# Attention output split straight into the tokens' tiles, and the first MoE's output weight converted where its factors are made

## The chip, the cores and the metric

One NeuronCore of a Trainium2 chip runs the whole program in one launch. The metric is the device time of one execution in microseconds; for the kernel before it is 955.79 us, the median of three runs (955.52 to 956.56).

## The reference, cut to what matters

Attention over 4 batches, 8 heads, 576 positions, head size 64, with a decay from the cumulative log of f, causal; its output, transposed to 2304 tokens by 512, goes through two MoE layers of width 2048 without routing. The MoE weights arrive as 64-bit floats, all else as float32.

```python
scores = where(causal, -1e9, scale * q @ k.T + cum[:, :, :, None] - cum[:, :, None, :])
attn = softmax(scores)                       # 4 x 8 x 576 x 576
x = (attn @ v).transpose(0, 2, 1, 3).reshape(2304, 512)
h = x @ moe_w_in                             # 512 -> 2048
x = (h * clip(h + 3, 0, 6) / 6) @ moe_w_out  # 2048 -> 512
h = x @ moe2_w_in
out = (max(h, 0) + log1p(exp(-abs(h)))) @ moe2_w_out
```

## The kernel before, in words

**Numbers.** Products of the MoE layers keep float32 accuracy by splitting each operand into a high part, rounded to the matmul's float32r type by ScalarE, and a low part, the difference, by VectorE or GpSimd; a product is three matmuls (high x high, high x low, low x high). A 64-bit weight tile is turned to float32 in three steps (raw_weights, lines 855 to 895): ScalarE scales the upper word (889), VectorE shifts the lower (891) and combines both (892). Three of the four MoE products (the second of the first MoE and both of the second) use a 2 x 2 scheme with seven products instead of eight, so weights are first made into seven factors, high and low, by weights(m, o, p): unit p covers two 128-row tiles of the weight, its sums are on line 932, its splits on 961 and 964, and it lies in tile U[p].

**Stages.** (1) Attention, by pairs of heads, 16 pairs, four per batch: scores (s_job, line 616, contraction of 64 rows for each head), a running minimum on VectorE (638), exponentials on ScalarE (647), transposes on TensorE (t_job, 710, four groups TP0 to TP3 per head; the first tile of 64 rows is in TP3), copies (732), the product with v (pv_job, 757), and the norm into xs (765). (2) Woven with it, the first product of the first MoE in five blocks of 512 tokens (step_g, 1008; the last has 256), evicted by 1013 and 1014; blocks 0 to 2 run beside the attention, 3 and 4 after it. (3) The second product (step_c, 1256). (4) The second MoE's first product (step_a, 1112). (5) Its second (step_b, 1311), nine blocks of 256 tokens; each block sums over eight p into four banks, which combine (1226, 1229) adds up before the store of the output (1327).

**Where x goes.** A block of tokens lies in one of two halves of MX, XG(t) with t modulo 2, high and low parts. A batch has 576 tokens and a block 512, so blocks and batches are shifted. Only for batch 0 are the first 512 tokens split from xs right away (772, 773). Every pair's xs is stored whole to x_dram (774); load_g (985) fetches blocks 1 to 4 from there, and 991 and 992 split them.

**Weights.** Two staging tiles st[0], st[1] serve all conversions during the attention, in the order in which the operations are created: 16 tiles of moe_w_in (weights_g), 16 of moe_w_out, and 16 of moe2_w_in, the latter two stored as float32 to wf_dram (899) and loaded again by weights (920). Two more staging tiles and U[1], U[2] exist once the attention's tiles are closed (open_m2). U[3] to U[7] hold the first product's weights until its last blocks have read them.

**Order.** Nothing is left to run-time scheduling. Each operation has a due time `at`, worked out from the numbers in PLAN; Work.order simulates the engines with assumed costs, gives every operation an engine, a bank and a place in its engine's queue, and each engine runs its queue in that order. All DMAs but a few are issued by SP. So a changed cost or due time moves the order of everything.

```python
best_way: min over engines of begin + cost
next op of an engine: among those that can start earliest, the one with the least `at`
```

Of the kernel before, what the change touches and what calls it, by code (L numbers as in the profile page):

```python
# [13 lines left out]
P = 128  # L14
# [37 lines left out]
    pc=78.633,  # L52
    pp=1626.916,
    pv=0,
    bend=[1.119, 1.0, 1.0, 0.9],
    b0=47.858,
    T0=59.215,
    D1=96.614,
    D2=81.65,
    D3=81.326,  # L60
    D4=70.932,
    gap=16.562,
    gap2=18.0,
    gap3=23.337,
    cA=1.111,
    SA=5.521,
    SC=4.964,
    SB=2.386,
    iva=9.172,
    nwarm=18,  # L70
    sp=0.871,
    evb=-0.48,
    u0=6.93,
    u1=47.121,
    u2=5.548,
    u3=2.95,
    fx=-1.856,
    ul=20.0,
    c1=9.498,
    c2=13.359,  # L80
    c3=23.635,
    cvw=0,
    ldw=48.152,
    xa=-3.322,
    xs=-1.161,
    ga=4.306,
    tsp=-10.459,
    xat=36.251,
    xl=1.582,
    rel=32.858,  # L90
    wfrom=7.28,
    lv0=7.543,
    lq1=4.785,
    decst=1.735,
    capH=5,
# [3 lines left out]
    slv=0,  # L99
    lat=1.649,  # L100
# [200 lines left out]
def attention_two_moe_kernel(  # L301
# [295 lines left out]
    def s_job(pn, i, idx, at):  # L597
# [27 lines left out]
        for ti, a, c, o, q0, r, y, _, _ in todo:  # L625
            for h in heads:
                par, bk = sets[h], bks[h, y]
                if c == q0 + r:
                    def hide(h=h, q0=q0, r=r):
                        blk = T["W"][z][h][:r, q0:q0 + r]  # L630
                        nc.gpsimd.affine_select(out=blk, in_=blk, compare_op=ALU.is_ge, fill=-1e9 / scale, base=0, pattern=[[-1, r]], channel_multiplier=1)  # L631

                    op(("pool", 2.0 * r + 40, hide), w=[("W", z, h, ti)], at=at, name="hide")
# [51 lines left out]
    def t_job(pn, i, idx, at):  # L685
# [26 lines left out]
        op(("pe", 109.0 * len(blocks), go), r=list(rd), w=[bk], banks=[bk], at=at, name=f"TP{idx}",  # L712
# [26 lines left out]
    def pv_job(b, hp, idx, at):  # L739
# [58 lines left out]
    def attention():  # L798
# [10 lines left out]
        for n in range(len(specs) + 1):  # L809
            for i in range(2):  # L810
# [16 lines left out]
                if not cur:  # L827
                    return
                if i == 0:
                    if n + 1 < len(specs):  # L830
                        load_v(*specs[n + 1], when(0.9))
                else:
# [6 lines left out]
                prev = (*specs[n], i)  # L839
# [137 lines left out]
    def load_g(t, at):  # L977

        a0, n = GB[t]
        done = 0  # L980
        while done < n:
            b, o = divmod(a0 + done, S)
            cnt = min(n - done, S - o)
            for c in range(NC):
                dma(lambda b=b, o=o, cnt=cnt, done=done, c=c: nc.sync.dma_start(out=XG(t)[1][:, c, done:done + cnt].bitcast(F32), in_=x_dram[b][c, :, o:o + cnt]),
                    4 * P * cnt, r=[("xd", b, c)], w=[("X", t % 2, c)], at=at + 0.1 * c, name="loadx")
            done += cnt
        for c in range(NC):
            def xt(c=c):
                return [x[:, c, 0:n] for x in XG(t)]  # L990
            op(("act", act(n, False), lambda xt=xt: nc.scalar.activation(out=xt()[0], in_=xt()[1].bitcast(F32), func=ACTF.Copy)), w=[("X", t % 2, c)], at=at + 0.1 * c, name="xh")
            op2(either(n, lambda e, xt=xt: e.tensor_tensor(xt()[1], xt()[1].bitcast(F32), xt()[0].bitcast(F32), op=ALU.subtract)), w=[("X", t % 2, c)], at=at + 0.1 * c, name="xl")
# [458 lines left out]
```

## Time and profile before

| | us |
|---|---|
| median of three runs | 955.79 |
| the profiled execution, device time | 956.72 |
| its span | 954.9 |
| TensorE busy in the span | 929.1 |
| VectorE busy | 698.9 |
| ScalarE busy | 541.5 |
| GpSimd busy | 100.8 |
| DMA, MB moved | 185.95 |

Busy times count instructions that run on an engine; matmuls are pipelined, so a busy TensorE is not one at its peak. A row of the view by stretches gives the busy time of the engines in one stretch with the count of instructions in brackets, the TensorE clock that was granted (1.00 is full), the share of time in which the DMA engines were busy and the rate. In a timeline, square brackets give the idle time ahead of an instruction and what ended it.

### The profile page before, as it was taken

To read this page: it belongs to the slowest core of one execution; us is meant where nothing else is said; L and a number is where in the kernel's file an instruction comes from. 1 tells how busy PE (TensorE), PEld (TensorE's weight loads), DVE (VectorE), ACT (ScalarE), POOL (GpSimd) and SP (SyncE) were. 2 spreads that over 40 slices of the span, in tenths; PEclk is the share of its full clock that TensorE was granted. 3 is DMA by queue.
4 is the path that set the end of the run, shared out by engine and by line. 5 is a ranking of instruction groups with operands and counts; after the bars stand their busy time and mean duration, and the time that the engine had idled before them with its cause. 6 is when DMAs were issued, how large, how long until landed. Compare 5 with 4: busy or idle time off the path is not lost.

```text
span 954.9 us, 18734 instructions
## 1 busy us (share of the span) xinstructions
PE 929.1 (97%) x6772; PEld 827.2 (87%) x6772; DVE 698.9 (73%) x1548; ACT 541.5 (57%) x1082; POOL 100.8 (11%) x238
## 2 busy tenths in 40 slices
PE   7989999989999999999999999999999999999997
PEld 5657667766767788899999999999999999999997
DVE  6757666556566478599898799969635888887785
ACT  5868666656567655453454355867666754333341
POOL 4322111111111011002003101000000000000000
PEclk9999999999999999999999999999999999999999
DMA  9897988896987798654634366699724544443441
GB/s 184 195 203 191 249 218 220 214 272 200 238 248 252 243 311 265 225 163 147 185 117 155 111 199 181 214 364 314 250 100 152 183 161 134 151 137 112 133 134 67
DMA packets 205982, 185.95 MB, mean 195 GB/s; under 512 B 105344, under 2 KB 152576, under 8 KB 205888
## 3 DMA queue, kind: packets, MB, share of 16 engines
q1 hardware_dynamic: 203264, 184.38, 65.3%
q8 instruction: 53, 0.87, 0.4%
q10 hardware_dynamic: 2624, 0.37, 0.3%
q14 instruction: 41, 0.34, 0.1%
HBM read 120.07 MB, written 64.63 MB: 193 GB/s over the span
## 4 chain that ended last, share of the span: by engine, by line
PE 73%; DVE 11%; DMA 9%; ACT 3%; issue 2%; SPq 1%; POOL 0%; ACTq 0%; DVEq 0%; POOLq 0%
PE bank L1008 19%; PE bank L1311 19%; PE bank L1112 14%; PE bank L1256 10%; PE bank L710 4%; PE bank L757 3%; PE bank L616 3%; DVE XO L1213 3%; DMA st<-in_moe_w_out_dram 2%; DVE U L964 2%; DMA GR<-g_dram 2%; DMA st<-in_moe_w_in_dram 2%; DMA kr<-in_k_dram 1%; DVE HY L1229 1%; ACT pt L732 1%
## 5 line engine op out<-in xcount | busy, mean ns | idle before, releaser
L1008 PE MATMUL bank<-MX,U 128*128 128x512 f32 (+1 forms) x960 | 235.7, 387 | 3.7 <-DVE stats L638 2.4
L1008 PEld LDWEIGHTS bank<-MX,U 128*128 128x128 f32 x960 | 158.8, 190 | 39.9 <-issue 9.0
L1311 PE MATMUL bank<-U,MX 128*128 128x256 f32 x1512 | 179.9, 281 | 0.0
L1311 PEld LDWEIGHTS bank<-U,MX 128*128 128x128 f32 x1512 | 179.6, 189 | 0.0
L1256 PE MATMUL bank<-XO,U 128*128 128x256 f32 x1344 | 159.2, 280 | 0.5 <-DVE XO L1213 0.5
L1256 PEld LDWEIGHTS bank<-XO,U 128*128 128x128 f32 x1344 | 158.4, 189 | 0.9 <-DVE XO L1213 0.7
L1112 PE MATMUL bank<-MX,U 128*128 128x288 f32 x672 | 92.4, 297 | 1.3 <-ACT HY L1128 0.9
L1112 PEld LDWEIGHTS bank<-MX,U 128*128 128x128 f32 x672 | 90.3, 188 | 2.7 <-ACT HY L1128 1.4
L1112 PE MATMUL bank<-XO,U 128*128 128x288 f32 x672 | 91.7, 297 | 0.2 <-DVE HY L1131 0.2
L1112 PEld LDWEIGHTS bank<-XO,U 128*128 128x128 f32 x672 | 90.4, 188 | 0.7 <-DVE HY L1131 0.5
L1013 ACT ACTIVATE HY<-bank,half 128x512 f32<-128x512 f32 x80 | 50.0, 641 | 49.1 <-PE bank L1008 44.2
L631 POOL TENSOR_SCALAR_AFFINE_SELECT w<-w 128x128 f32<-128x128 f32 (+1 forms) x160 | 51.6, 326 | 238.2 <-DVE stats L638 126.1
L732 ACT ACTIVATE pt<-bank 128x384 f32<-128x384 f32 (+2 forms) x127 | 58.8, 496 | 29.5 <-PE bank L710 26.8
L1014 DVE SCALAR_TENSOR_TENSOR HY<-HY,bank 128x512 f32<-128x512 f32 x80 | 49.4, 631 | 35.0 <-ACT HY L1013 34.1
L1131 DVE TENSOR_TENSOR HY<-HY,bank 128x288 f32<-128x288 f32 x96 | 42.9, 450 | 36.3 <-PE bank L1112 34.8
L1128 ACT ACTIVATE HY<-bank 128x288 f32<-128x288 f32 x128 | 50.4, 406 | 27.2 <-PE bank L1112 26.8
L616 PE MATMUL bank<-KT,QT 64*128 64x288 f32 (+4 forms) x384 | 59.9, 424 | 2.9 <-DVE QT L570 1.3
L964 DVE TENSOR_TENSOR U<-st,U 128x1024 fp32r<-128x1024 f32 (+1 forms) x48 | 52.8, 1113 | 5.0 <-ACT U L961 4.9
L961 ACT ACTIVATE U<-st 128x1024 fp32r<-128x1024 f32 (+1 forms) x48 | 45.0, 948 | 19.5 <-DVE st L932 9.9
L1153 ACT ACTIVATE HY<-HY 128x576 f32<-128x576 f32 x64 | 43.7, 684 | 20.5 <-DVE HY L1131 17.0
L616 PEld LDWEIGHTS bank<-KT,QT 64*128 64x128 f32 x384 | 32.1, 187 | 26.5 <-issue 8.0
L1209 ACT ACTIVATE MX<-GR 128x768 fp32r<-128x768 f32 x36 | 30.2, 838 | 42.0 <-PE bank L1311 42.0
(147 smaller groups left out, 1303.3 us busy)
## 6 DMA issues: line engine op xcount, KB each, us to landing
GR<-g_dram SPq DMA_DIRECT2D x72, 512.0 KB
g_dram<-HY SPq DMA_DIRECT2D x32, 576.0 KB
st<-in_moe_w_in_dram SPq DMA_DIRECT2D x32, 512.0 KB
g_dram<-HY SPq DMA_DIRECT2D x64, 256.0 KB
st<-in_moe_w_out_dram SPq DMA_DIRECT2D x32, 512.0 KB
wf_dram<-st SPq DMA_DIRECT2D x48, 256.0 KB
st<-wf_dram SPq DMA_DIRECT2D x48, 256.0 KB
w<-dec_dram SPq DMA_DIRECT2D x30, 288.0 KB
```

The costliest lines, as they stand in the source:

```text
L616: nc.tensor.matmul(bank[bks[h, y].i][:, o:o + c - a], T["Q"][z][h * D:h * D + D, q0:q0 + P], T["K"][z][h * D:h * D + D, a:c], start=lead, ...
L631: nc.gpsimd.affine_select(out=blk, in_=blk, compare_op=ALU.is_ge, fill=-1e9 / scale, base=0, pattern=[[-1, r]], channel_multiplier=1)
L732: e.activation(out=place(i, j, a, c), in_=src(), func=ACTF.Copy)
L961: op(("act", act(n * h, False), lambda src=src, to=to: nc.scalar.activation(out=to(0), in_=src(), func=ACTF.Copy)), r=rd, w=w, at=at, name ...
L964: e.tensor_tensor(to(1), src(), to(0).bitcast(F32), op=ALU.subtract)
L1008: nc.tensor.matmul(bank[bk.i][:, 0:n], w, x, start=(c == 0 and y == 0), stop=(c == NC - 1 and y == 2))
L1013: op(("act", act(n, True, 1) + 10, lambda: nc.scalar.activation(out=g, in_=bank[bk.i][:, 0:n], func=ACTF.Relu, scale=1.0 / 6.0, bias=half) ...
L1014: op(("dve", dve(n), lambda: nc.vector.scalar_tensor_tensor(out=g, in0=g, scalar=1.0, in1=bank[bk.i][:, 0:n], op0=ALU.min, op1=ALU.mult)), ...
L1112: nc.tensor.matmul(bank[bks[b].i][:, 0:HA], wa[u][:, c], xa[v][:, c], start=(nm in ("P1", "P2", "P5") and c == 0 and y == 0), stop=(c == 1 ...
L1128: op(("act", act(HA, True) + 30, lambda: nc.scalar.activation(out=to(q), in_=bp(), func=ACTF.Copy)), r=new, banks=[ba], w=[("H", i, q)], a ...
L1256: nc.tensor.matmul(bank[bks[b].i][:, o * 256:(o + 1) * 256], *ops, start=(p == 0 and o == 0 and y == 0), stop=(p == NPR - 1 and y == 2), s ...
L1311: nc.tensor.matmul(bank[bks[b].i][:, o * 256:(o + 1) * 256], ga[u], wa[v], start=(p == 0 and o == 0 and y == 0), stop=(p == NPR - 1 and y ...
```

## The change

Six things change, and with them the order of all operations, since it is worked out anew.

1. Each pair's output is split from xs straight into the block of its batch: batch b's first 512 - 64 b tokens go to the block b, high by ScalarE and low by VectorE or GpSimd. Only the remaining 64 (b + 1) tokens are stored to x_dram, and load_g fetches them for block b + 1 in two transfers (three of the four column groups, then the last). A half of MX now has two keys for each column group, for the part from xs and for the part from DRAM, and every product of the block reads both. To keep the dependencies in order, attention is a generator that yields after each batch, and the block's products are created between.
2. moe_w_out is no longer converted into wf_dram during the attention; weights(0, 1, p) loads the 64-bit tiles and converts them in the staging tiles ahead of its sums.
3. The first tile's transposes use 64 rows and a 64 x 64 identity instead of 128 x 128; the planner's cost for one is 55 ns instead of 109.
4. In the last block of stage 5 the products of the last two p are interleaved (P1 of both, P6 of both, ...), and its output is stored in three parts: one row half whole, the other in two halves of 128 KB.
5. The first weight's loads are created ahead of the attention, so they no longer follow the store of the decays.
6. Most numbers of PLAN change; the planner's cost of one causal mask on GpSimd rises by 50 ns.

```diff
 PLAN = dict(
...
-    b0=47.858,
+    b0=45.976,
     T0=59.215,
-    D1=96.614,
-    D2=81.65,
+    D1=102.897,
+    D2=77.724,
...
-    u1=47.121,
+    u1=49.035,
...
-    ldw=48.152,
+    ldw=37.258,
...
-    capH=5,
+    capH=4,
...
-    lat=1.649,
+    lat=2.309,
 )
...
             for p0, ti, k0 in blocks:
-                nc.tensor.transpose(acc[:, p0:p0 + P], T["P"][par][ti][:, k0:k0 + P], ident)
+                r = CUT[ti][1]
+                nc.tensor.transpose(acc[:, p0:p0 + r], T["P"][par][ti][0:r, k0:k0 + P], ident[0:r, 0:r])
...
-        if b == 0:
-            xh, xl = (XG(0)[z][:, hp] for z in range(2))
-            op(("act", act(TB, False), lambda: nc.scalar.activation(out=xh, in_=X()[:, 0:TB], func=ACTF.Copy)), r=xk, w=[("X", 0, hp)], at=at - K["xat"], name="xh")
-            op2(either(TB, lambda e: e.tensor_tensor(xl, X()[:, 0:TB], xh.bitcast(F32), op=ALU.subtract)), r=xk, w=[("X", 0, hp)], at=at - K["xat"], name="xl")
-        dma(lambda: nc.sync.dma_start(out=x_dram[b][hp], in_=X()), 4 * P * S, r=xk, w=[("xd", b, hp)], at=at, name="storex")
+        o, n = S * b - TB * b, TB * (b + 1) - S * b
+        xh, xl = (XG(b)[y][:, hp, o:TB] for y in range(2))
+        op(("act", act(n, False), lambda: nc.scalar.activation(out=xh, in_=X()[:, 0:n], func=ACTF.Copy)), r=xk, w=[("X", b % 2, hp, 0)], at=at - K["xat"], name="xh")
+        op2(either(n, lambda e: e.tensor_tensor(xl, X()[:, 0:n], xh.bitcast(F32), op=ALU.subtract)), r=xk, w=[("X", b % 2, hp, 0)], at=at - K["xat"], name="xl")
+        dma(lambda: nc.sync.dma_start(out=x_dram[b][hp, :, n:S], in_=X()[:, n:S]), 4 * P * (S - n), r=xk, w=[("xd", b, hp)], at=at, name="storex")
...
     def load_g(t, at):
-        a0, n = GB[t]
...
+        b = t - 1
+        s0 = TB * t - S * b
+        n = S - s0
+        for c0, c1 in ((0, NC - 1), (NC - 1, NC)):
...
+                nc.sync.dma_start(out=XG(t)[1][:, c0:c1, 0:n].bitcast(F32), in_=x_dram[b][c0:c1, :, s0:S].rearrange("c p s -> p c s"))
...
-            op(("pe", 3 * 119.0, go), r=[("unit", p, group(fz))] + [("gf", 1, i, 3 * (az > 2), s) for s in range(2)], w=[bks[b]], banks=[bks[b]], at=mb_at(t, p, x / 7), name="b" + nm,
+            op(("pe", 3 * 119.0, go), r=[("unit", p, group(fz))] + [("gf", 1, i, 3 * (az > 2), s) for s in range(2)], w=[bks[b]], banks=[bks[b]], at=mb_at(t, p, x / 7) if t < NT // NG - 1 or p < NPR - 2 else mb_at(t, NPR - 2, (2 * x + p % 2) / 7), name="b" + nm,
...
-        for h in range(2):
+        cuts = [(1, 0, 2), (0, 0, 1), (0, 1, 2)] if t == NT // NG - 1 else [(0, 0, 2), (1, 0, 2)]
+        for h, y0, y1 in cuts:
...
-    converts(0, 1, BLK[1] - K["c1"], BLK[2] - K["c1"], 2)
+    pass
     converts(1, 0, BLK[2] - K["c2"], BLK[3] - K["c2"], 2)
...
+    for t in attention():
...
-    weights(0, 1, 0, c_at(0, 0) - K["u1"] - 30, 0, False)
+    weights(0, 1, 0, c_at(0, 0) - K["u1"] - 30, 0, True)
...
-        weights(0, 1, p, c_at(0, p) - K["u1"] - 15, p % 2 * 2, False)
+        weights(0, 1, p, c_at(0, p) - K["u1"] - 15, p % 2 * 2, True)
```

## Rows read from the trace of the kernel before

**Rows 1.** Busy time by stretches: attention (two), the rest of stage 2, stage 3
```profile
20.00:140.00 120.00, 110.64 (x720) 76.60 (x718) 81.20 (x267) 88.57 (x243) 28.18 (x76) 0.97 0.86 211
140.00:340.00 200.00, 196.30 (x1213) 142.98 (x1210) 116.03 (x339) 126.77 (x319) 25.22 (x78) 0.99 0.83 236
340.00:400.00 60.00, 60.00 (x344) 52.33 (x344) 44.36 (x89) 29.39 (x49) 5.90 (x3) 1.00 0.85 282
400.00:580.00 180.00, 179.06 (x1500) 177.56 (x1499) 162.40 (x289) 85.63 (x105) 17.52 (x18) 1.00 0.50 152
```
**Rows 2.** The same view in steps of 20 us
```profile
120.00:140.00 20.00, 18.18 (x96) 12.54 (x96) 11.20 (x37) 13.26 (x36) 3.04 (x9) 0.91 0.82 228
```
**Rows 3.** Timeline of TensorE, instructions behind an idle stretch
```profile
131.59 0.33 PE L710 MATMUL bank<-ident,p3b 128*128 128x128 f32 x1 [1.82 <-DVE stats L638]
...
197.30 1.65 PE L1008 MATMUL bank<-MX,U 128*128 128x512 f32 x3 [2.39 <-DVE stats L638]
```
**Rows 4.** Chain of waits: start, us, what
```profile
190.36 5.82 DMA st<-in_moe_w_out_dram
...
230.27 6.52 DMA st<-in_moe_w_out_dram
```
**Rows 5.** DMA view, 20 to 340 us
```profile
DMA packets 119086, 72.43 MB, mean 226 GB/s; under 512 B 85837, under 2 KB 100356, under 8 KB 119050
...
st<-in_moe_w_in_dram SPq DMA_DIRECT2D x24, 512.0 KB
...
st<-in_moe_w_out_dram SPq DMA_DIRECT2D x16, 512.0 KB
```
**Rows 6.** Timeline of VectorE: a norm, the next batch's first, a split after its load
```profile
164.20 0.49 DVE L765 TENSOR_TENSOR xs<-bank,ivb 128x320 f32<-128x320 f32 x1
...
181.51 0.43 DVE L765 TENSOR_TENSOR xs<-bank,ivb 128x256 f32<-128x256 f32 x1
182.47 0.69 DVE L992 TENSOR_TENSOR MX<-MX 128x512 fp32r<-128x512 f32 x1 [0.53 <-ACT MX L991]
```
**Rows 7.** Timeline of SP's issues: the last loads of x for block 1
```profile
175.94 1.00 SPq L985 DMA_DIRECT2D MX<-x_dram  x2
```
**Rows 8.** Timeline of ScalarE: the last eviction of block 0
```profile
161.19 0.69 ACT L1013 ACTIVATE HY<-bank,half 128x512 f32<-128x512 f32 x1 [0.39 <-PE bank L1008]
```
**Rows 9.** Stretches, instructions of line 892 alone: VectorE busy, clock, DMA
```profile
140.00:285.00 145.00, 11.03 (x16) 0.99 0.85 229
285.00:400.00 115.00, 12.41 (x18) 1.00 0.81 268
```
**Rows 10.** Groups by form: busy us, mean ns of one, idle before
```profile
L891 DVE TENSOR_SCALAR st<-st 128x512 uint32<-128x512 uint32 x64 | 27.4, 428 | 24.7 <-DMA st<-in_moe_w_in_dram 12.5 <-DMA st<-in_moe_w_out_dram 12.2
```
**Rows 11.** Stretches in stage 3, columns as in rows 1
```profile
420.00:460.00 40.00, 39.06 (x325) 38.30 (x324) 38.43 (x70) 18.69 (x22) 5.13 (x5) 1.00 0.55 171
460.00:500.00 40.00, 40.00 (x342) 40.00 (x341) 35.30 (x64) 19.68 (x26) 0.74 (x1) 1.00 0.45 134
```
**Rows 12.** Chain of waits: G matmuls behind scores, between transposes; transposes alone
```profile
107.00 0.90 PE bank L1008 x3
...
122.50 0.70 PE bank L1008 x3
...
329.61 0.33 PE bank L710 x3
```
**Rows 13.** Groups by form: weight loads of the scores and of transposes
```profile
L616 PEld LDWEIGHTS bank<-KT,QT 64*128 64x128 f32 x384 | 32.1, 187 | 26.5 <-issue 8.0 <-DVE stats L638 8.0 <-ACT pt L732 4.3
...
L710 PEld LDWEIGHTS bank<-ident,pc 128*128 128x128 f32 x120 | 14.2, 142 | 7.7 <-DVE stats L638 2.6 <-DVE xs L765 1.6 <-issue 0.8
```
**Rows 14.** Timeline of the tail, all engines
```profile
943.79 5.72 PE L1311 MATMUL bank<-U,MX 128*128 128x256 f32 x47
...
948.56 2.75 DVE L1229 TENSOR_TENSOR HY<-HY,bank 128x256 f32<-128x256 f32 x7 [5.96 <-ACT HY L1226]
951.00 0.81 SPq L1327 DMA_DIRECT2D out_dram<-HY  x2
```

More of the change, by code (lines that the diff above doesn't have):

```diff
@@ L98 @@
     slp=0,
-    slv=0,
-    lat=1.649,
+    slv=26.051,
+    lat=2.309,
 )
@@ L709, in go @@
             for p0, ti, k0 in blocks:
-                nc.tensor.transpose(acc[:, p0:p0 + P], T["P"][par][ti][:, k0:k0 + P], ident)
-        op(("pe", 109.0 * len(blocks), go), r=list(rd), w=[bk], banks=[bk], at=at, name=f"TP{idx}",
+                r = CUT[ti][1]
+                nc.tensor.transpose(acc[:, p0:p0 + r], T["P"][par][ti][0:r, k0:k0 + P], ident[0:r, 0:r])
+        op(("pe", sum(109.0 if CUT[b[1]][1] == P else 55.0 for b in blocks), go), r=list(rd), w=[bk], banks=[bk], at=at, name=f"TP{idx}",
            after=[("PT", i, t[0], t[1]) for t in todo])
@@ L826, in attention @@
                         pv_job(*prev[:2], idx, at - K["tsp"])
-                if not cur:
-                    return
-                if i == 0:
+                if cur and i == 0:
                     if n + 1 < len(specs):
                         load_v(*specs[n + 1], when(0.9))
-                else:
+                elif cur:
                     inv_job(n, when(1.0) - K["iva"])
@@ L977, in load_g, with xt @@
     def load_g(t, at):
-        a0, n = GB[t]
[L980 to L992, printed above, removed]
+        b = t - 1
+        s0 = TB * t - S * b
+        n = S - s0
+        for c0, c1 in ((0, NC - 1), (NC - 1, NC)):
+            k = [("X", t % 2, c, 1) for c in range(c0, c1)]
+            dma(lambda c0=c0, c1=c1: nc.sync.dma_start(out=XG(t)[1][:, c0:c1, 0:n].bitcast(F32), in_=x_dram[b][c0:c1, :, s0:S].rearrange("c p s -> p c s")),
+                4 * P * n * (c1 - c0), r=[("xd", b, c) for c in range(c0, c1)], w=k, at=at, name="loadx")
+            def xt(c0=c0, c1=c1):
+                return [x[:, c0:c1, 0:n] for x in XG(t)]
+            m = n * (c1 - c0)
+            op(("act", act(m, False), lambda xt=xt: nc.scalar.activation(out=xt()[0], in_=xt()[1].bitcast(F32), func=ACTF.Copy)), w=k, at=at + 1, name="xh")
+            op2(either(m, lambda e, xt=xt: e.tensor_tensor(xt()[1], xt()[1].bitcast(F32), xt()[0].bitcast(F32), op=ALU.subtract)), w=k, at=at + 1, name="xl")
     ngb = [0]
@@ L1008, in go @@
                     nc.tensor.matmul(bank[bk.i][:, 0:n], w, x, start=(c == 0 and y == 0), stop=(c == NC - 1 and y == 2))
-            op(("pe", 3 * (0.4495 * n + 3.2), go), r=[("W1", ft, 0), ("W1", ft, 1), ("X", t % 2, c)], w=[bk], banks=[bk], at=at, name=f"G{t}.{ft}", seq="s" if c == 0 else None)
+            op(("pe", 3 * (0.4495 * n + 3.2), go), r=[("W1", ft, 0), ("W1", ft, 1)] + [("X", t % 2, c, y) for y in range(2)], w=[bk], banks=[bk], at=at, name=f"G{t}.{ft}", seq="s" if c == 0 else None)
         g = HY[0][:, i * TB:i * TB + n]
@@ L1332, in attention_two_moe_kernel @@
         op(("pe", 213.0, lambda: nc.tensor.matmul(bank[0][:, 0:P], ident, ident)), r=["ident"], w=[wb], banks=[wb], at=-10.0, name="warm")
-    attention()
-    last_att = list(wk.ops)
+    for ft in range(NF):
+        weights_g(ft)
     wk.mark = ()
@@ L1370, in attention_two_moe_kernel @@
             freed(on_tile[made], [("unit", made, 0), ("unit", made, 1)])
-            weights(0, 1, made, c_at(0, made) - K["u1"], made % 2 * 2, False)
+            weights(0, 1, made, c_at(0, made) - K["u1"], made % 2 * 2, True)
             made += 1
-    freed([("X", z, c) for z in range(2) for c in range(NC)], xkeys("M"))
+    freed([("X", z, c, y) for z in range(2) for c in range(NC) for y in range(2)], xkeys("M"))
     freed([("g", i) for i in range(4)], obs)
```

80 lines of the change are left out of this document (42 added, 38 removed).

## The prediction

> **What bounds the kernel now.** The execution behind the profile took 956.72 us on the device, 954.9 of them span; the median of the runs shown is 955.79, so I work out a difference and put it on both. First I read the stretches by stage [rows 1]. From 400 us on TensorE is never free for more than a per cent: 179.06 busy of 180 in the second products of the first MoE. 340 to 400 is full. Only the attention, woven with the first MoE's first products, has holes: 9.36 idle of 120 (20 to 140 us) and 3.70 of 200 (140 to 340), 13.1 together. A hole also costs afterwards: the 20 us with the idle stretch at 131.59 have a granted clock of 0.91, a part of them at 1.2 instead of 2.4 GHz [rows 2]; with two more such stretches (0.91 from 60 us, 0.92 from 180) that is 20 x (0.09 + 0.09 + 0.08) = 5.2 us of work (the stages' mean clocks of 0.97 and 0.99 give 5.6). So 18.3 us is the most that smoother attention could give back.
>
> Then I ask what ends the holes. The two longest after 100 us, 1.82 and 2.39 us, wait for VectorE's row statistics (line 638) [rows 3], and the chain of waits puts ahead of the second of them a load of a staged weight that takes 5.82 us; ahead of 1.30 us more at 236 to 239 stands another, of 6.52 us [rows 4]. The engine reads its queue in order: a conversion whose weight has not landed (line 891) stands in front of the attention's reductions. Between 20 and 340 us the DMA moves 72.43 MB [rows 5] and its engines are busy 0.83 to 0.86 of the time [rows 1]. This is a stage where TensorE has little slack and DMA decides where it waits.
>
> **The x path.** Before, a pair's normed output goes to DRAM and comes back. For the last pair of the second batch the norm ends at 164.69, the last loads are issued at 175.94, and the low part of the split starts at 182.47 [rows 6, 7]: 18 us, in which the next G block can only hold open banks. After, ScalarE and VectorE split straight out of xs; of 0.69 us each at 512 columns these two instructions were paid before too, only after the load, so their sum is nil: 24 pairs of instructions instead of 20, each shorter. What goes is DMA: stores of 576 tokens per batch become 64 (b+1), so 2304 x 2048 B = 4.72 MB become 640 x 2048 B = 1.31, and loads of 1792 tokens (3.67 MB) become 1.31: 5.8 MB less, and SP issues 16 + 8 transfers instead of 16 + 28. What is late next is the split's own dependency: batch b writes the half of MX that block b-2 read. Batch 2's first pair is normed at 181.51, 20 us after the last eviction of block 0 begins [rows 6, 8], so I cost that wait at nothing; if cover went, an ACT queue with exponentials behind it would wait.
>
> **The weight path.** 16 conversions of moe_w_out (loads of 512 KB, conv on ACT and DVE, store and reload of 256 KB each) leave the attention [rows 5]. Their place, 140 to 285 us, held 16 of the combining steps; the stretch 285 to 400 held 18, those of moe2_w_in [rows 9]. Staging has two buffers and is filled in order of creation, so moe2_w_in should move up into the vacated place, and moe_w_out comes after it, at the factors. VectorE there gets 16 x (0.43 + 0.69) = 17.9 us [rows 9, 10] and loses 18 x the same = 20.1: about nil, beside 15.6 us free in 340 to 400 [rows 1]. 8.4 MB of traffic, the store and reload of 16 x 256 KB, disappears. With x, and with 16 conversions fewer before 340 (where 40 ran, 16 of w_out and 24 of w_in [rows 5]; now some 34, as unit 0 and a few more come early), the attention moves about 72.4 - 5.8 - 6 x 0.5 - 8 x 0.26 = 61.5 MB, 15% less.
>
> How much of the holes that closes I can't read off; the bounds are 0 and 18.3. The waits that end in a staged load or stand right behind one are 1.82 + 2.39 + 1.30 = 5.5 us, and two of the three stretches of low clock follow them (1.8 + 1.6): 8.9. As the conversions of moe2_w_in now stand where those of moe_w_out stood, the in-order wait itself stays, only the load is shorter; I take half, **-4.5 us**.
>
> Block 0 of the second products needs a unit of factors every 5 us (42 matmuls of 0.117, by 342 in 40 us). At 420 to 460 it ran 325 matmuls where the next 40 us ran 342 [rows 11]: 17 x 0.117 = 2.0 us lost now, with VectorE 38.43 of 40 busy. Units 0, 2, 4 and 6 hung on buffers that moe2_w_in held until 392; they can now be early, but each takes a load of twice the bytes and 2.24 us of VectorE more. Between -2 and +4 us; **-0.5**.
>
> **The half-height transposes.** 32 blocks (one in each group TP3) become 64 rows by 64 columns moving instead of 128. Full ones take 0.11 us each (0.33 for three) [rows 12]. If time went by moving columns alone, 32 x 0.055 = 1.7 us go. Against it: three G matmuls take 0.70 us between transposes, but 0.90 next to the scores' 64-row matmuls, with the same 512 columns [rows 12]: going into another row shape and back costs 0.19 to 0.20 us. A 64-row block within 128-row work pays that too: 32 x (0.19 - 0.055) = +4.3 us; if nothing is saved either, 32 x 0.19 = +6.1. From -1.7 to +6.1; some of the blocks already stand next to scores or PV and pay half. The nearest row is the 64-row scores, so I take **+3.5 us**, on TensorE's path, since in this stage nothing hides it.
>
> Whether even the 0.055 are saved depends on the weight load. Scores load 64 x 128 in 187 ns, transposes 128 x 128 in 142 [rows 13]: half the rows don't load faster. The Trainium skill, in "TensorE: Matmul & The Clock Gate", section "LDWEIGHTS (loading the stationary operand)", says the same: the time goes by columns, not by the contraction rows. By that rule the half block's load is as long as before, the saving is nil and the total 2.6 us worse than mine.
>
> **The tail.** The last matmul ends at 949.51, VectorE's seven additions end at 951.31, two stores are issued from 951.00 to 951.81 [rows 14]. They start late because bank 0 closes only 5 x 0.357 us before the end (five more products of three matmuls, 0.119 each by the same row's 47). Interleaved, P1 and P6 are complete 10 x 0.357 = 3.6 us before it, five additions lie beside matmuls, and one of 0.4 remains behind the last. The last store is issued near 950.0 instead of 951.4, and is half as large: **-1.5 us** (-0.8 to -2.2). It needs the last unit's factors one step earlier, and they are there: in the last 6 us no matmul waits.
>
> **Sum.** -4.5 - 0.5 + 3.5 - 1.5 = -3.0 us: 953.7 against the profiled 956.72, 952.8 against the median.
>
> **Rivals.**
> (a) The transposes cost what their columns say: -4.5 - 0.5 - 1.7 - 1.5 = -8.2, 947.6. For it: the transposes' load is shorter than others' [rows 13]. Against it: 0.70 and 0.90 [rows 12].
> (b) The half transposes save nothing and pay every switch, +6.1: -4.5 - 0.5 + 6.1 - 1.5 = -0.4, 955.4; no change. The section named above stands behind the first half of it.
> (c) Slower: the row-shape switches, +4.3 for all 32, with nothing from the DMA's relief, because moe2_w_in's conversions block VectorE just where moe_w_out's did: +4.3 - 1.5 = +2.8, 958.6. It decides once the relief is under 0.9 us. For it: order and planner's constants are new everywhere, and holes elsewhere may open.
> (d) The units come late: moe2_w_in does not move up, 17.9 us go onto 340 to 400, where 15.6 are free; 2.3 spill into block 0, where each lost step shows, beside the 2.0 lost there: +4 in place of -0.5, 957.3.
>
> **Chances and range.** Mine 0.40, (a) 0.17, (b) 0.10, (c) 0.20, (d) 0.13. What a measurement of this kernel tells from no change is about 0.2%, 1.9 us: 953.9 and 957.7. Faster: most of mine (0.32), (a), a little of the others: 0.54. Same 0.22. Slower: (c) and half of (d), and what of mine goes wrong: 0.24. My own case spans 948 to 956. The range reaches from below (a), with two thirds more relief, to above (c) with +6.1: 945 to 961.
>
> **What would show it.** Relief: TensorE's idle time from 20 to 340 falls from 13.1 towards 9, loads of staged weights get shorter, the granted clock dips less often. Weights: conversions of moe2_w_in end before 320, those of moe_w_out lie from there to 430, and 420 to 460 holds 325 matmuls or more. Transposes: G matmuls or transposes next to a 64-row block start about 0.1 us later than next to a full one; if the spacing falls to 0.055 with no gap, (a). Tail: last store's issue within 1 us of the last matmul. The prediction is wrong if a new hole of over 3 us opens in the attention, if block 0 starves, or if G matmuls wait on the x split.

## The result and the profile after

The changed kernel takes 962.89 us, the median of four runs; the kernel before took 955.65 in the same session. The ratio is 1.0073, with an interval of 1.0046 to 1.0099: slower by 7 us, where 3 us less were forecast, and outside the range. The profiled execution took 962.57 us, 960.8 of them span: 5.9 more than the span before. The differences below are made on these two executions.

First the stretches, with the columns of [rows 1]: us, busy time and count of TensorE, weight loads, VectorE, ScalarE and GpSimd, granted clock, DMA share, GB/s.

```profile
20.00:140.00 120.00, 115.23 (x722) 79.67 (x719) 85.57 (x274) 90.96 (x250) 25.84 (x73) 0.95 0.81 196
140.00:340.00 200.00, 194.77 (x1194) 138.39 (x1192) 111.16 (x334) 121.58 (x312) 24.43 (x79) 0.98 0.68 192
340.00:400.00 60.00, 57.36 (x316) 48.47 (x313) 55.55 (x96) 35.59 (x55) 12.05 (x14) 1.00 0.70 232
400.00:580.00 180.00, 180.00 (x1488) 178.05 (x1487) 147.50 (x264) 78.60 (x99) 20.12 (x18) 1.00 0.47 142
```

In the second row the DMA share fell from 0.83 to 0.68 and TensorE's idle time rose from 3.70 to 5.23 us: the traffic went and the holes stayed. Idle time from 20 to 340 us is 4.77 + 5.23 = 10.0 (13.1 before), but the clock is lower in both rows: 120 x 0.05 + 200 x 0.02 = 10.0 us of work, where it was 5.6. The stretch 340 to 400 has 2.64 us of holes where it had none, with VectorE 55.55 of 60 busy instead of 44.36. In steps of 20 us, these two carry most of the lost clock [rows 2]:

```profile
20.00:40.00 20.00, 18.36 (x111) 13.09 (x109) 13.19 (x46) 13.80 (x42) 3.25 (x12) 0.79 0.86 177
220.00:240.00 20.00, 16.98 (x91) 12.09 (x89) 7.57 (x23) 8.61 (x24) 1.81 (x6) 0.83 0.81 224
```

TensorE's timeline shows what stood ahead of them, and a third hole later; these answer to [rows 3].

```profile
31.57 1.87 PE L616 MATMUL bank<-KT,QT 64*128 64x288 f32 x4 [1.27 <-DVE stats L638]
...
224.41 0.33 PE L711 MATMUL bank<-ident,p1b 128*128 128x128 f32 x1 [1.42 <-DVE stats L638]
...
227.37 0.36 PE L711 MATMUL bank<-ident,p0b 64*128 64x64 f32 x1 [1.60 <-DVE stats L638]
...
271.81 0.81 PE L616 MATMUL bank<-KT,QT 64*128 64x320 f32 x4 [1.88 <-DVE stats L638]
```

The chain of waits over 214 to 230 us answers to [rows 4]: the load is now one of moe2_w_in (the view leaves out the 2), and no shorter (5.82 and 6.52 before).

```profile
218.50 2.09 DMA wf_dram<-st
220.59 0.02 issue
220.60 6.06 DMA st<-in_moe_w_in_dram
```

VectorE's timeline shows the queue that TensorE hangs on: it stands twice at a conversion (L892), with the row statistics (L638) right behind; at 270.56 the attention's statistics stand behind the split of an x that came from DRAM (L992).

```profile
223.80 0.43 DVE L892 TENSOR_SCALAR st<-st 128x512 uint32<-128x512 uint32 x1 [2.47 <-DMA st<-in_moe_w_in_dram]
224.14 0.21 DVE L638 CUSTOM_DVE_ANT_0 pc<-bank,w 64x64 f32<-64x64 f32 x1
...
226.76 0.43 DVE L892 TENSOR_SCALAR st<-st 128x512 uint32<-128x512 uint32 x1 [2.40 <-DMA st<-in_moe_w_in_dram]
...
270.56 0.76 DVE L992 TENSOR_TENSOR MX<-MX 128x576 fp32r<-128x576 f32 x1 [4.02 <-ACT MX L991]
271.23 0.51 DVE L638 CUSTOM_DVE_ANT_0 pc<-bank,w,stats 128x288 f32<-128x288 f32 x1
```

The DMA view of 20 to 340 us [rows 5]: 10.5 MB less, as forecast (61.5 MB), with 4 loads of moe_w_out instead of 16.

```profile
DMA packets 118054, 61.89 MB, mean 193 GB/s; under 512 B 86274, under 2 KB 103682, under 8 KB 118018
...
st<-in_moe_w_in_dram SPq DMA_DIRECT2D x29, 512.0 KB
...
st<-in_moe_w_out_dram SPq DMA_DIRECT2D x4, 512.0 KB
```

The combining steps (now L893) before and after 285 us [rows 9], and the start of the second products [rows 11]:

```profile
140.00:285.00 145.00, 9.66 (x14) 0.98 0.72 197
285.00:400.00 115.00, 13.42 (x20) 1.00 0.63 206
```

```profile
420.00:460.00 40.00, 40.00 (x340) 40.00 (x339) 30.20 (x55) 15.03 (x18) 6.47 (x5) 1.00 0.40 125
460.00:500.00 40.00, 40.00 (x341) 40.00 (x340) 33.76 (x61) 19.02 (x24) 1.85 (x1) 1.00 0.53 157
```

In TensorE's timeline the starts of transposes show the 64-row blocks [rows 12]: full after full follows in 0.11 us (22.08, 22.19, 22.30), a half one behind a full one in 0.20 (22.30 to 22.50), a full one behind a half one in 0.20 (23.07 to 23.27).

```profile
22.08 0.27 PE L711 MATMUL bank<-ident,p2b 128*128 128x128 f32 x1
22.19 0.27 PE L711 MATMUL bank<-ident,p3b 128*128 128x128 f32 x1
22.30 0.27 PE L711 MATMUL bank<-ident,p4b 128*128 128x128 f32 x1
22.50 0.64 PE L711 MATMUL bank<-ident,p 64*128 64x64 f32 x3
23.07 0.27 PE L711 MATMUL bank<-ident,p0b 64*128 64x64 f32 x1
23.27 0.33 PE L711 MATMUL bank<-ident,p1b 128*128 128x128 f32 x1
```

Their weight loads, by form (busy us, mean ns), are 136 ns for 64 rows and 149 for 128 [rows 13]; the tail answers to [rows 14].

```profile
L711 PEld LDWEIGHTS bank<-ident,pc 128*128 128x128 f32 x112 | 14.0, 149 | 3.2 <-ACT pd L647 0.8
...
L711 PEld LDWEIGHTS bank<-ident,pc 64*128 64x128 f32 x8 | 1.1, 136 | 2.2 <-issue 1.1 <-ACT pt L733 1.0 <-ACT U L974 0.2
```

```profile
939.83 16.55 PE L1311 MATMUL bank<-U,MX 128*128 128x256 f32 x138
...
956.42 1.08 DVE L1229 TENSOR_TENSOR HY<-HY,bank 128x256 f32<-128x256 f32 x3 [0.33 <-PE bank L1311]
956.87 1.30 SPq L1328 DMA_DIRECT2D out_dram<-HY  x3
```

### The profile page after: what moved, and what is told of

It reads as the page before. It is cut to its first block, busy times and chain, and to the rows that moved or that the text cites. A ratio compares the mean times of both kernels' runs of the same rounds, so it can differ in the third digit from the quotient of the medians.

```text
span 960.8 us, 18597 instructions
## 1 busy us (share of the span) xinstructions
PE 938.2 (98%) x6772; PEld 831.4 (87%) x6772; DVE 702.1 (73%) x1545; ACT 543.2 (57%) x1082; POOL 108.3 (11%) x249
## 4 chain that ended last, share of the span: by engine, by line
PE 84%; DVE 6%; DMA 6%; ACT 1%; issue 1%; POOL 1%; SPq 0%; DVEq 0%; POOLq 0%; ACTq 0%
PE bank L1311 19%; PE bank L1008 18%; PE bank L1112 17%; PE bank L1256 15%; PE bank L711 6%; PE bank L616 4%; PE bank L758 4%; DMA st<-in_moe_w_in_dram 2%; DVE XO L1213 2%; DVE U L965 1%; DMA g_dram<-HY 1%; PE bank L1333 1%; DMA w<-dec_dram 1%; DMA GR<-g_dram 1%; DVE HY L1014 1%
## 5 line engine op out<-in xcount | busy, mean ns | idle before, releaser
L1008 PE MATMUL bank<-MX,U 128*128 128x512 f32 (+1 forms) x960 | 238.8, 388 | 3.0 <-DVE HY L1014 2.0
L733 ACT ACTIVATE pt<-bank 128x448 f32<-128x448 f32 (+2 forms) x123 | 58.4, 498 | 25.6 <-PE bank L711 24.7
L1209 ACT ACTIVATE XO<-GR 128x768 fp32r<-128x768 f32 x36 | 30.3, 841 | 51.1 <-PE bank L1256 35.9
L1213 DVE TENSOR_TENSOR MX<-GR,MX 128x768 fp32r<-128x768 f32 x36 | 34.7, 964 | 30.2 <-ACT MX L1209 30.2
```

The costliest lines, as they stand in the source:

```text
L733: e.activation(out=place(i, j, a, c), in_=src(), func=ACTF.Copy)
L1008: nc.tensor.matmul(bank[bk.i][:, 0:n], w, x, start=(c == 0 and y == 0), stop=(c == NC - 1 and y == 2))
L1209: op(("act", act(cnt, False), lambda src=src, dst=dst: nc.scalar.activation(out=dst(0), in_=src(), func=ACTF.Copy)), r=rd, w=[("gf", m, i, ...
L1213: e.tensor_tensor(dst(1), src(), dst(0).bitcast(F32), op=ALU.subtract)
```

## The experiments

Ratios are to the kernel before, run beside each, with 95% intervals. "Loss" is TensorE's idle time up to the end of its last PV product (the product with v), plus half of the time at 1.2 GHz there; it is 23.0 us before and 24.7 after, with the last PV product ending at 332.8 and 340.2.

Losses and ends of stages are read from one execution of each kernel, and they vary. Two pairs of kernels have the same order in every queue up to the last block: the kernel before and e9 lose 23.0 and 21.9 us, with the last PV product ending at 332.8 and 330.4; e12 and e15 lose 22.6 and 19.5, at 333.6 and 330.3. So a difference of 3 us in the loss is no difference between kernels; the ratios, from 4 to 12 runs of each, are the firmer numbers.

### The half-height transposes

The changed kernel in its own order with full transposes, and the kernel before in its own order with half ones:

```diff
-tensor.transpose(acc[:, p0:p0 + r], T["P"][par][ti][0:r, k0:k0 + P], ident[0:r, 0:r])   # e1_full: changed kernel
+tensor.transpose(acc[:, p0:p0 + P], T["P"][par][ti][:, k0:k0 + P], ident)
```

> The changed kernel with the 32 half-height transposes issued as full 128 x 128 ones again; the order of every queue is that of the changed kernel. Theory 'row shape': in the trace of the changed kernel a half block starts 0.203 us after the matmul ahead instead of 0.109, and the next full block again 0.203 after it, so 30 x 0.094 + 32 x 0.094 = 5.8 us go: 962.9 - 5.8 = 957.1, and the span of the attention (last product with v) from 340.2 to about 334.5. Rival 'columns': halving the moving columns saved 32 x 0.055 = 1.7 us and the attention is longer for another reason (new holes): 964.6. Rival 'waits take it': the attention waits on VectorE anyway, so shorter transposes only lengthen the waits: 961 to 963.

> The kernel before with the same 32 transposes at half height, nothing else, order of all queues as before. Row shape: +5.8 us, 961.4 to 961.5, if nearly all groups stand behind 128-row work. Columns: -1.7, 954. If e1 and this one agree in size with opposite signs, the term stands alone and doesn't hang on the rest of the change.

Measured: 957.53 us, 1.0022 [0.9999, 1.0045], against 1.0073 with half blocks; and 957.37, 1.0024 [1.0000, 1.0049], for half blocks alone. They cost in both directions, 0.0051 and 0.0024, the second at the edge of its interval. TensorE's work up to the last PV product (its end less the loss) grew with the half blocks by 4.9 us from e1 to the changed kernel and by 6.6 from before to e2, so in e2 part of the cost seems to have filled holes; how much, one execution can't tell (the profiled one took 954.70, the median is 957.37). And e1, which holds every other part of the change, is no faster than before: the expected gain is missing without them too.

### Is it the conversions' work?

In the changed order, VectorE's part of moe_w_out's conversion is left out and its load takes as many bytes of q (e3), then ScalarE's part too (e5), or the whole conversion of moe2_w_in (e4):

```diff
-op2(("dve", dve(n), lambda: nc.vector.scalar_tensor_tensor(
+op2(("dve", dve(n), lambda: None if (m, o) == (0, 1) else nc.vector.scalar_tensor_tensor(   # e4: (1, 0)
```

> The changed kernel in its order, without VectorE's two conversion steps of moe_w_out (32 instructions, 17.9 us of VectorE); the staged words are loaded from q in the same shape and size, so the outputs are not the reference's. Theory 'VectorE full': between 340 and 380 us it is busy 17.1 and 20.0 of 20 and G matmuls wait 2.6 us for the evictions of line 1014; without the steps these waits go and G ends 73 us after the last product with v instead of 76.7: -2.5 to -3.7 us, 959.2 to 960.4. Rival 'DMA': the evictions wait for stores of g (4.00 us in the chain of waits at 354.8) and loads of the factors, which don't change here: within 1 us of 962.9.

> The changed kernel in its order, without all three conversion steps of moe_w_out, ScalarE's too (words loaded from q in the same shape and size; outputs not the reference's). Without VectorE's two steps alone the stretch from the last product with v to the end of G stayed at 77.3 us (76.8 in the changed kernel, 73.0 before). Theory 'ScalarE's queue': G evictions (line 1013) stand behind conversions (line 890) whose 512 KB have not landed (4.1 and 1.4 us in the run with full transposes); without them the stretch falls to 73.5 to 75, the time by 2 to 3.5 us. Rival 'factor loads': VectorE and ScalarE stand at the first factors of G (loads of 6.5 to 7.5 us), which stay: the stretch stays above 76.

> The changed kernel in its order, without the three conversion steps of moe2_w_in (ACT's and VectorE's); the words are loaded from q in the same shape and size, stored and reloaded as before, so the outputs are not the reference's. Theory 'in order': the holes of 3.0 us at 224 to 227 and 2.2 at 271 to 278 and the low clock after the first (6.8 us at half) come from VectorE standing at a conversion whose weight hasn't landed; without it they go: 3.0 + 2.2 + 3.4 = -8 to -9 us, 954. Rival 'just work': only the instructions' own time goes, which TensorE does not see here: -1 to 0. Rival 'other waits': the next-latest thing in the same queue (loads of q and k, decays) ends the waits instead: -3 to -5.

Measured: 1.0061 [1.0041, 1.0081], 1.0085 [1.0062, 1.0107], 1.0080 [1.0055, 1.0104]; the changed kernel has 1.0073. Taking away work gives nothing. The stretch from the last PV product to the end of G (the first MoE's first product), 73.0 us before and 76.7 in the changed kernel, stays at 77.3 in e3 and 75.8 in e5. In e4 the holes at 224 us are gone, but one of 5.28 us stands at 263, behind the split of an x that SP began to load only at 263.19: the next wait was right behind. The lines are TensorE's and VectorE's.

```profile
268.71 1.44 PE L616 MATMUL bank<-KT,QT 64*128 64x320 f32 x4 [5.28 <-DVE stats L638]
...
267.46 0.76 DVE L992 TENSOR_TENSOR MX<-MX 128x576 fp32r<-128x576 f32 x1 [7.42 <-ACT MX L991]
```

### Is it the wait in order behind loads?

With full transposes, e6 holds the DRAM part of x of the last two blocks until the attention's planned end; e7 also lets the planner price the loads of moe_w_out at twice their bytes, e8 all staged loads; e10 is e8 without holding x.

```diff
-..., w=k, at=at, name="loadx")
+..., w=k, at=at, name="loadx", from_=BLK[3] if t > 2 else 0.0)     # e6, e7, e8
-dma(load, 8 * P * NC * P, w=[("stage", i), ("up", i)], ...
+dma(load, 16 * P * NC * P, w=[("stage", i), ("up", i)], ...         # e8, e10; e7: for (0, 1) alone
```

> The changed kernel with full transposes, and with the loads of x from DRAM for blocks 3 and 4 held in the plan until the attention's end, so that their splits leave the attention's queues (planned anew from there on). Theory 'split in the way': the hole before the scores at 268 to 272 us (2.0 us, 5.3 in the run without the conversions, there with 3.5 us of low clock after) comes from ScalarE and VectorE standing at lines 991 and 992 for a load that SP issues late behind k loads. It goes: 957.5 - 2 to 4 = 953.5 to 955.5. Rival: the reductions then wait for the next thing (decays, k): within 1 us of 957.5.

> As the run before, and the plan prices moe_w_out's staged loads at twice their bytes (5.8 us to landing instead of 4.0; the traces show 5 to 7.5), so conversions stand later in the queues of ScalarE and VectorE. If the loss after the attention is in-order waiting for loads, the stretch from the last product with v to the end of G falls from 77 to 73 to 75 and the time by 2 to 3 us against the run before. If it is the amount of work or of traffic there, it stays.

> As the run before, with all staged loads priced so, also those within the attention; the whole order is planned anew. In-order theory: the holes at 221 to 228 us behind two conversions go too, -3 us more or better. Rival: the plan's order elsewhere gets worse as loads take more of its DMA time, or the holes only move, as in the run without moe2_w_in's conversions: 0 to +4.

> The changed kernel with full transposes, and the plan prices every staged load at twice its bytes; x loads as in the changed kernel. The run that also held x back ended the attention at 330.3 us (336.4 with full transposes alone, 332.8 before) but lost 4 us waiting for x right after. Theory 'in order': the attention's holes come from conversions planned sooner than loads land; here the attention ends near 330, x is there, G takes 73 to 76: 957.5 - 5 = 951 to 953.5. Rival 'moved': the gain in the attention came from holding x back, or is lost again after it: 956 to 959.

Measured: 1.0103 [1.0081, 1.0125], 1.0073 [1.0050, 1.0095], 1.0042 [1.0027, 1.0058], 1.0017 [0.9998, 1.0037]. Prices nearer to the landing times close the holes at 221 to 271 us, and the last PV product ends at 331.6 in e10 instead of 336.4 in e1; yet the time is e1's, since 4 us went to a later stage (A, the second MoE's first product, takes 188.4 instead of 184.3). e6 moved the wait, and e7 hardly shortens it (82.8 us from the last PV product to the end of G, 84.7 in e6, where 73 to 75 were expected). In e6 TensorE stands still for 8.63 us after the attention, and ScalarE's timeline shows why, a conversion waiting for its load ahead of the split (L991) in the same queue.

```profile
344.62 0.68 ACT L890 ACTIVATE st<-st 128x512 f32<-128x512 f32 x1 [3.27 <-DMA st<-in_moe_w_out_dram]
345.95 0.68 ACT L890 ACTIVATE st<-st 128x512 f32<-128x512 f32 x1 [0.66 <-DMA st<-in_moe_w_out_dram]
346.84 0.94 ACT L991 ACTIVATE MX<-MX 128x576 fp32r<-128x576 f32 x2 [0.20 <-DMA MX<-x_dram]
```

The same pricing on the kernel before:

> The kernel before with one edit: the planner prices all loads of staged weights at twice the bytes, nearer to the 5 to 7.5 us that they are seen to take, so that conversions are placed later than their loads. If the in-order wait at a conversion is what makes the attention's holes, the holes behind staged loads (at 131 and 197 us) go and the attention ends 2 to 4 us earlier; time -1 to -3 us if the rest keeps it, 0 if it is lost again in the products behind, as it was in the changed kernel. Rival, that the holes have other releasers: attention end unchanged.

Measured: 1.0556 [1.0524, 1.0589], against the theory. The attention ends at 333.1, as before, and TensorE stands still for 51.7 us from 406: moe2_w_in's conversions, held back, run on to 450, ahead of the factors of the second products. So a later place for the conversions closes holes in one order and opens a far larger one in another; the landing time is not the cause by itself.

```profile
457.87 0.77 PE L1256 MATMUL bank<-XO,U 128*128 128x256 f32 x2 [51.74 <-issue]
```

### The parts one by one

e9 is the kernel before with the interleaved last block and the three-part store; e12 with moe_w_out converted at the factors; e15 with both; e13 is the change without its weight path and its half blocks, in the numbers that the planner had before: the x part, the tail and the order of creation (the planner's costs of a mask and of a half block stay those of the change).

```diff
-converts(0, 1, BLK[1] - K["c1"], BLK[2] - K["c1"], 2)               # e12, e15
-weights(0, 1, p, c_at(0, p) - K["u1"] - 15, p % 2 * 2, False)
+weights(0, 1, p, c_at(0, p) - K["u1"] - 15, p % 2 * 2, True)
+... if t < NT // NG - 1 or p < NPR - 2 else mb_at(t, NPR - 2, (2 * x + p % 2) / 7)   # e9, e15
```

> The kernel before with the last block's interleaved products and the output's store in three parts, nothing else; the order differs from before's only at the end. By the trace of the changed kernel the stretch behind the last product falls from 5.4 to 4.4 us and the last stage from 177.3 to 176.5: -1.0 to -1.8 of 955. Rival: the three smaller stores land no earlier: 0.

> The kernel before with moe_w_out converted at its factors, nothing else; PLAN as before, so the order is new from the first conversion on. If 16 conversions and 6 MB fewer relieve the attention: its idle and low-clock time (13.1 + 5.1 from 20 us) falls, -2 to -4 us. If they are replaced by those of moe2_w_in with the same waits and G loses 2 to 3 us after the attention behind loads (as in the changed kernel: 2.6): 0 to +2.

> The kernel before with the x path of the changed kernel (and its interleaved tail), full transposes, PLAN as before, moe_w_out through DRAM as before; the planner still counts 55 ns for a half block. If the x path alone helps: the attention ends some us before 332.8, 950 to 953 with the tail. If splits of the DRAM part stand in the attention's queues and cost holes: 955 to 959. With e12 it tells which half of the change brings the missing relief, and which the loss.

> The kernel before with two parts of the change: moe_w_out converted where its factors are made, and the last block's products interleaved with the three-part store. Full transposes, x by DRAM, the planner of before. My theory, that these two parts gain and add: alone they gave 0.9974 and 0.9979, together about 0.995, -4 to -5 us, 951 to 952; TensorE's tail near 4.7 us, attention end near 333. Rival, that the gain of the tail and that of the conversion are the same microseconds (the last units come late): 0.997 to 0.998, no more than either alone.

Measured: e9 0.9979 [0.9955, 1.0003]; e12 0.9974 [0.9955, 0.9993]; e13 1.0088 [1.0058, 1.0118]; e15 951.28 us, 0.9959 [0.9939, 0.9979]. e15 beats both kernels, and e12 alone is clear of 1. The tail alone is not (its interval reaches 1.0003), though the stretch behind the last product is 0.7 to 0.8 us shorter in both pairs that differ in it (5.40 to 4.70, 5.00 to 4.24). That the two gains add fits e15, but so does a tail worth less: the intervals of e12 and e15 overlap. The x part with its order of creation costs 8 us, with holes from 29 to 78 us and a loss of 30.6.

### The order of creation

One thing in that part was in no term of mine. The first MoE's weights are now created ahead of the attention, so that the load of block 0's first weight no longer waits for the store of the decays. In the planner that wait is not only lost, it is turned round: the load still reads the key ("dec") that the store writes, so the store, created later, waits for the load. SP's timeline has two 512 KB loads ahead of the rows of k, one before, and it issues the store and the first reload of the decays later (13.39 and 19.87 us, 9.60 and 14.65 before); the kernel after, then the kernel before:

```profile
5.80 1.14 SPq L870 DMA_DIRECT2D st<-in_moe_w_in_dram  x2
7.06 3.99 SPq L534 DMA_DIRECT2D kr<-in_k_dram  x4
...
13.39 0.44 SPq L797 DMA_DIRECT2D dec_dram<-w  x1
...
19.87 1.55 SPq L575 DMA_DIRECT2D w<-dec_dram  x2
```

```profile
5.82 0.58 SPq L869 DMA_DIRECT2D st<-in_moe_w_in_dram  x1
...
9.60 0.47 SPq L796 DMA_DIRECT2D dec_dram<-w  x1
...
14.65 0.98 SPq L575 DMA_DIRECT2D w<-dec_dram  x2
```

Giving the wait back to e1 (e16), to e13 (e17) and to the whole change (e18), and taking it from the kernel before (e21):

```diff
 def attention():
-    decays()                       # e16, e17, e18
+decays()
 for ft in range(NF):
     weights_g(ft)
-raw_weights(i, 0, 0, ft, at, ["dec"] * (ft == 0))     # e21
+raw_weights(i, 0, 0, ft, at)
```

> The changed kernel with full transposes in the same order, and the decays' store created ahead of the first MoE's weights again, so that the first weight loads wait for it as in the kernel before. Theory, that the loss of the x part sits in the start (two 512 KB loads ahead of the k and r loads, holes and half clock at 18 to 50 us): those holes go, 3 to 5 us less than the same kernel without this edit (957.5), so 953 to 955. Rival, that the split of x from xs and the DRAM part of x in the attention's queues cost it: the early holes may go, the time stays at 956 to 959.

> The kernel with the x part on its own (x split straight from xs, interleaved last block, the planner of before, moe_w_out by DRAM, full transposes), now with the decays' store ahead of the weights. Without that edit it ran at 1.0088. Theory, that the order of creation is the loss: 0.998 to 1.001, and the holes at 29 to 78 us are gone. Rival, that the x split itself is: 1.005 to 1.009, with holes behind VectorE and ScalarE at the split and its DRAM loads left.

> The whole change, half transposes included, with one thing undone: the decays' store is created ahead of the first MoE's weights, so that the load of block 0's first weight again waits for it. Theory, that the lost wait is what the change pays for: from 962.9 down by 5 to 6 us as with full transposes (957.5 to 952.8), to 956 to 958, ratio to the kernel before 1.000 to 1.003, which is what the 64-row blocks cost over e16_dec. Rival, that the early holes close only with the particular order of e16_dec: 960 or more.

> The kernel before with only that wait taken away: the load of the first weight no longer depends on the decays' store (another order, the same numbers in the planner). Theory: two 512 KB loads ahead of the k rows, holes at 18 to 80 us, attention end 4 to 8 us later, ratio 1.004 to 1.008. Rival, that it is not the wait but how each new order happens to fall: any change of the planner's input moves the time by some us either way, and this one may be anywhere from 0.997 to 1.003 without the two early loads standing out.

| kernel | ratio | last PV ends | loss, us | MB, 20 to 340 us |
|---|---|---|---|---|
| before | 1 | 332.8 | 23.0 | 72.4 |
| after | 1.0073 | 340.2 | 24.7 | 61.9 |
| e18, after with the wait | 1.0038 [1.0020, 1.0056] | 336.9 | 19.2 | 62.0 |
| e1, after with full transposes | 1.0022 | 336.4 | 25.8 | 62.0 |
| e16, e1 with the wait | 0.9961 [0.9941, 0.9981] | 330.6 | 18.9 | 63.4 |
| e13, x part | 1.0088 | 340.9 | 30.6 | 67.8 |
| e17, e13 with the wait | 0.9974 [0.9954, 0.9995] | 326.4 | 16.2 | 69.6 |
| e12, weight path | 0.9974 | 333.6 | 22.6 | 68.1 |
| e21, before without the wait | 0.9975 [0.9954, 0.9996] | 328.6 | 16.4 | 73.4 |

Within the change the wait is worth 0.0061, 0.0114 and 0.0035 (the last only just clear of noise): my theory by three runs. e21 goes against it. Its timeline of SP has the same two early loads,

```profile
5.75 1.13 SPq L869 DMA_DIRECT2D st<-in_moe_w_in_dram  x2
7.00 3.84 SPq L534 DMA_DIRECT2D kr<-in_k_dram  x4
10.93 0.52 SPq L796 DMA_DIRECT2D dec_dram<-w  x1
...
15.57 0.92 SPq L575 DMA_DIRECT2D w<-dec_dram  x2
```

and yet it is faster than before, with holes from 20 to 80 us that never cost the clock:

```profile
20.00:40.00 20.00, 16.32 (x125) 10.64 (x125) 12.74 (x46) 14.70 (x43) 4.60 (x13) 1.00 0.84 163
40.00:60.00 20.00, 18.30 (x140) 11.92 (x136) 15.44 (x61) 17.09 (x54) 7.04 (x21) 1.00 0.75 184
60.00:80.00 20.00, 17.32 (x125) 12.59 (x122) 12.89 (x38) 13.34 (x37) 2.36 (x9) 1.00 0.98 195
```

And in e16 the clock loss that was to go stands at 40 to 60 us, at a new hole of 3.12 us:

```profile
40.00:60.00 20.00, 16.77 (x98) 10.87 (x98) 12.09 (x42) 12.67 (x38) 5.14 (x14) 0.74 0.89 185
```

So the early loads are not the cause by themselves. But e21 takes the wait away, where the change turns it round, and there a rival is left. The first reload of the decays is issued at 19.41 to 19.87 us in the changed kernel, e1 and e13, and at 14.65 to 15.57 in every kernel that they are compared with here (before, e16, e17, e18, e21), so late decays fit the three pairs within the change (the 2.4 us between e21 and the kernel before they leave open). By the chain of waits the hole at 31.57 us in the changed kernel ends behind a load of the decays (issued at 26.74, 3.44 us), but so does one at 30.51 in e21 (24.45, 4.73 us). No run tests it: the change with the key taken out would.

What the edit does each time is to give the planner another input, from which it writes another order for every engine; the pairs hold the same work and differ by 2.4 us (before, e21), 5.8 (e1, e16) and 10.9 (e13, e17). That the order makes these differences is shown; which property of it does, the late decays or another, is open. e21 also says how far to trust the parts: with no work moved it gains as much (0.9975) as the weight path in e12 (0.9974).

## Why the prediction was wrong, step by step

By the two profiled executions, +5.9 us of span where -3.0 was forecast:

| step | forecast | measured |
|---|---|---|
| relief of the attention | -4.5 | +1.7 (loss 23.0 to 24.7) |
| half-height transposes | +3.5 | +5.8 (62 x 0.094, by the spacing) |
| factors, block 0 | -0.5 | +0.8 (rest of G +3.7, second products -2.9) |
| tail | -1.5 | -1.0 (last product to span's end, 5.4 to 4.4) |
| the other MoE products (A and B) | none | -1.4, not followed up |

**The relief failed**, the step "I take half, -4.5 us". The bytes went as worked out, and the loss did not follow: +1.7 is less than two executions of one order differ by, but a relief of 4.5 it is not. The table of kernels shows that the loss does not go by bytes: e12 moved 4.3 MB less and lost as much as before, e21 moved 1 MB more and lost 6.6 us less. The prediction itself said that the in-order wait stays and only the load gets shorter; the load on the chain did not get shorter (6.06 us), and by the chain it still starts only when the store out of the same buffer has landed (218.50 to 220.59). The bounds, 0 to -18.3, were one-sided: no bound was set for an order that loses more, though rival (c) noted that the order "is new everywhere". What is shown of the order is that e16, the same work with full transposes and the decays' store created first, came to 0.9961, some 6 us better than e1. With the order of creation undone, e16 and e18 lose 18.9 and 19.2 us (one execution each), 4 less than before, which is about the size forecast. So the step failed in that it let the relief depend on the traffic alone; the new order of creation, the fifth item of the change, was in no term.

The clock's share of the bound was also taken for a property of the kernel. e9, in the same order, has a clock of 1.00 at 120 to 140 us, where the kernel before has 0.91 [rows 2], and 0.91 at 20 to 40, where that one has 1.00.

```profile
120.00:140.00 20.00, 18.41 (x116) 12.59 (x112) 12.56 (x40) 14.07 (x38) 3.39 (x10) 1.00 0.81 229
```

**The transposes** were mis-sized, and rival (b) had them: a half block costs 0.203 - 0.109 = 0.094 us more on entry and as much on exit, over 32 blocks some 5.8 us. The prediction's 0.19 for both switches is what the spacing shows as the whole cost, so its 0.055 for the columns has to go. It also let some blocks pay half for standing next to scores: 2 of the 32 stand right behind them, while 14 stand behind a product of G and pay the same there (0.328 us to the half block, 0.234 to a full one). The rule of the Trainium skill that was weighed there ("TensorE: Matmul & The Clock Gate", "LDWEIGHTS (loading the stationary operand)") agrees with the trace: 136 ns for a load of 64 rows, 149 for one of 128. What they cost in time, 0.0051, 0.0077 (e16 to e18) and 0.0024, is 4.9, 7.4 and 2.3 us; with intervals of some 2 us on each ratio only the largest and the smallest differ, and those narrowly; that holes grow or shrink around the blocks may be why, but is not shown.

**The weight path** went as described: moe2_w_in moved up (14 and 20 combining steps before and after 285 us, its last loads issued by 304), and 420 to 460 holds 340 matmuls, not 325. The conversions of moe_w_out then lie on 340 to 400, where VectorE had 15.6 us free. G's remainder there took 3.7 us longer and the second products 2.9 less; the longer remainder is not the conversions' work, since it stays without it (e3, e5), and its cause is open. Alone the weight path came to 0.9974 (e12), where rival (d) had a loss.

**The x path** was costed at nothing but bytes. Its splits take the place of others, as said; with the wait given back, e17 holds it and the tail at 0.9974, no worse than the tail alone at 0.9979. What was missed is that the splits of the remainders from DRAM stand in queues read in order, as at 270.56, and that the order of creation changes too.

**The tail** gained 1.0 of 1.5: the last store's issue ends at 958.17, 1.8 us after the last product (956.38), since three stores take 1.30 us of SP where two took 0.81.

**Of the marks set**, a hole of over 3 us did not open in the attention; several of 1.3 to 2.2, some with lost clock behind them, did. Idle time from 20 to 340 us did fall towards 9 (10.0), but the loads of staged weights got no shorter and the clock lost more.

## What to carry to other kernels

Bytes removed from a stage need not buy time: what counts is the wait that ends last there. Where an engine stands in order at a conversion, ask what stands in that place after. A change that makes a planner write a new order can move the time by that alone: here 2 to 11 us for the same work, as large as the gains sought, so measure each part under more than one order before calling it good or bad, and put that swing on both sides of the range. When creation is moved in a planner that finds dependencies by keys, look whether a wait is gone or turned round. And take a loss from several executions: here two of one order were 3 us apart. A shorter matmul of another row shape between full ones can cost more than the full one.

## What the hardware showed that I had not expected

- Between matmuls of 128 and 64 rows TensorE pays on both sides: 0.203 instead of 0.109 us into a 64-row transpose, and 0.203 into the next full one. Weight loads of 64 and of 128 rows take 136 and 149 ns.
- Shorter idle time costs the clock in one place and not in another: from 20 to 40 us the changed kernel had 1.64 us idle and a mean clock of 0.79, e21 3.68 us idle and a clock of 1.00. Nor does one order fix it: from 120 to 140 us the kernel before was idle for 1.82 us at a clock of 0.91, e9 for 1.59 us at 1.00.
- Removing work from VectorE and ScalarE (e3, e5) did not shorten the kernel (1.0061 and 1.0085, against 1.0073), though the chain of waits over 336 to 380 us names VectorE's conversion steps for a tenth of it.
